# Logits copied out in their own step, the slot sum divided after the experts, a shorter merge of four groups

## The chip, the cores and the metric

The kernel runs on one core of a Trainium2 chip. The metric is device time in microseconds, 398.91 us as the median of three runs before the change. The engines are named as the profile names them: PE (TensorE matmul, with PEld its weight loads), DVE (VectorE), ACT (ScalarE), POOL (GpSimd) and SP (the queue that issues all transfers here).

## What is computed

The reference, cut to what matters (sizes: 4 sequences of 576 tokens, 8 heads of 64, so N = 2304 tokens of width 512; 8 experts with 4 slots each, 32 slots; inner width 1024; feed-forward width 2048):

```python
# attention in a window of 64 tokens, causal; output x: [2304, 512]
logits = x @ phi                                     # [N, 32]
d = exp(logits - logits.max(0)); d /= d.sum(0) + 1e-9   # over the tokens, per slot
slot_input = d.T @ x                                 # [32, 512]
for e in range(8):                                   # 4 slots each
    slot_out[e] = maximum(slot_input[e] @ w1[e], 0) @ w2[e]
c = exp(logits - logits.max(1)); c /= c.sum(1) + 1e-9   # over the slots, per token
y = c @ slot_out                                     # [N, 512]
h = y @ w_in; out = (h * sigmoid(1.702 * h)) @ w_out
```

## The kernel before, in words

**Attention.** A list `work` of 20 steps is run by one loop (line 618), five for each sequence `b`: a step for each of its four pairs of heads and, second among the five, a short one for the tail of the sequence. The loop is a pipeline written out by hand, and every engine executes its own instructions in the order of the program. In pass `i` PE does the scores of step i (`emit_s`, lines 324 and 338), the transposes of step i-1 (`emit_t`, line 359), the transposes of the attention output of step i-2 (`xt_step`, lines 415 and 421) and the product with V of step i-1 (`emit_pv`, line 374). ACT does the exponentials (`emit_e`, line 350) and copies transposes out of PSUM (lines 360 and 430), DVE the row maxima (line 343) and the normalisation (`emit_norm`), POOL scales and shifts inputs as they land (lines 218, 238 and 241).

**Routing.** The softmax over the tokens is built online, one sequence at a time (`routing(b)`), and its parts are hung into the loop by the tables `early` (between `emit_e(i, 0)` and `xt_step`) and `late` (after `emit_e(i, 1)`). For b = 0, 1, 2 the order is: in step 5b + 6, late, `all_logits` (lines 480 to 491) on PE; in step 5b + 7, early, `lmax` on DVE (lines 500 to 505: running maximum and the change of it) and `dexp` on ACT (line 510 the exponential, with its sum; 513; and line 515, a copy of the raw logits into the SBUF strip `ls`); late in the same step `dtr`, which transposes the exponentials and the raw logits on PE (lines 522 and 523); in step 5b + 8 `slots` on PE (539 and 542) and `gather` on DVE, which adds to `acc`. The softmax over the slots (`norm`, `side`) hangs in later.

**PSUM banks.** Eight banks are handed out in rings: `s` three, `v` two, `m` three. `emit_t` takes two of `m` in each step, `xt_step` one, `all_logits` one, `dtr` two, `slots` one. A tile waits until the one that had its bank has been read. In step 5b + 7 the ring gives `xt_step` the bank that `all_logits` took one step before, and the last reader of that bank is the copy in line 515. After the loop the rings are `s` [1, 0], `t` [2, 7], `v` [3, 4], `m` [5, 6].

**The merge.** For the fourth sequence the same is done outside the loop (lines 688 to 742). The partitions of `acc` hold four groups of the 32 slots, each with its own running maximum and sum, and these are merged: PE transposes the maxima (line 701), DVE reduces them, PE spreads the result (708), DVE and ACT make the factor of each group (712 and 713). Then the sums are brought together (717, 719, PE at 721), the reciprocal is taken (722, 724), the factors are made (725, 726), `acc` is scaled (727), the last `slots` are added (734), and PE sums the four groups and transposes in one (738); DVE copies the result, `siT`, which stands in the buffer `phis` (741). Between these stand the parts of `c` for three sequences (`sides[b][0]` to `[2]`: line 439 on PE, 448 on ACT, 453 on DVE).

**Experts and feed-forward.** `emit_w1` (lines 753 and 757) makes four rounds over the 16 tiles of w1, `emit_ht` transposes the hidden values, `emit_w2` (line 792) goes over the 16 tiles of w2, `so_copy` (line 842) copies the sum out of PSUM, `so_turn` (848) transposes it. The feed-forward stage then takes the rest of the time, in 48 steps of matmuls (lines 948 and 975) with the activation on ACT.

**Transfers.** All are issued by SP, in the order of the program, each when its buffer is free: in each attention step one pair's q and k (512 KB), its v (256 KB), and one or two 1 MB tiles of w1; w2 goes first into the space that attention leaves (`arena`), and from the seventh tile on into the slots that a round of `emit_w1` frees.

Of the kernel before, what the change touches and what calls it, by code (L numbers as in the profile page):

```python
# [15 lines left out]
ACTF = mybir.ActivationFunctionType  # L16
ALU = mybir.AluOpType
# [3 lines left out]
B, H, S, D = 4, 8, 576, 64  # L21
# [53 lines left out]
def attention_softmoe_ffn(  # L75
# [12 lines left out]
    nc = tc.nc  # L88
# [12 lines left out]
    pa = s1.tile([128, 2048], F32, tag="pa", name="pa")  # L101
# [7 lines left out]
    def bank(tag, shape=(128, 512), dtype=F32):  # L109
        ring = rings[tag]  # L110
        ring.append(ring.pop(0))
        return psp.tile(list(shape), dtype, tag=f"b{ring[-1]}", name=tag)
# [10 lines left out]
    acc = cst.tile([128, DM], F32, name="acc")  # L123
# [17 lines left out]
    def load_w(n=1):  # L141
        for _ in range(n):
            if plan:
                lst, src, i, d = plan.pop()
                t = wslot() if d is None else dslot(d)
                v = src[i].rearrange("p (a f) -> p a f", a=4)
                for c in HALVES if plan == [] else (slice(0, 512),):
                    nc.sync.dma_start(out=t[:, :, c], in_=v[:, :, c])
                lst.append(t)
# [133 lines left out]
    ls = rawt[:, LS0:LS0 + 192]  # L283
# [11 lines left out]
    i4m = i4.rearrange("p j s -> p (j s)")  # L295
# [141 lines left out]
    def c_tile(p, l):  # L437
        for j in range(4):
            nc.tensor.matmul(
                p[32 * j:32 * j + 32], l, ident, start=True, stop=True, tile_position=(0, 32 * j))  # L440
# [30 lines left out]
    def routing(b):  # L471
        st = {}
# [5 lines left out]
        def logits(lp, kks, rest):  # L478
            if rest:
                nc.tensor.matmul(  # L480
                    lp[:, 128:192], negs[:, 0:128], negs[:, 128:192], start=True, stop=True)
                for kk in range(KD):
                    nc.tensor.matmul(
                        lp[0:32, 128:192], phis[:, kk, :], xT[:, kk, 512:S],
                        start=(kk == 0), stop=(kk == KD - 1), tile_position=(0, 0))
            for kk in kks:
                for t in range(4):
                    nc.tensor.matmul(
                        lp[32 * t:32 * t + 32, 0:128], phis[:, kk, :],
                        xT[:, kk, 128 * t:128 * t + 128],  # L490
                        start=(kk == 0), stop=(kk == KD - 1), tile_position=(0, 32 * t))
            st["lp"] = lp[:, 0:192]

        def all_logits():
            logits(bank("m"), range(KD), True)

        def lmax():

            m = sp.tile([128, 1], F32, tag="mrun", name="mrun")
            nc.vector.tensor_reduce(out=m, in_=st["lp"], axis=AX.X, op=ALU.max, negate=True)  # L500
            if b:
                nc.vector.tensor_tensor(out=m, in0=m, in1=run["m"], op=ALU.min)
                al = sp.tile([128, 1], F32, tag="al", name="al")
                nc.vector.tensor_tensor(out=al, in0=m, in1=run["m"], op=ALU.subtract)
                st["al"] = al
            run["m"] = m

        def dexp():
            s = sp.tile([128, 1], F32, tag="srun", name="srun")
            nc.scalar.activation(  # L510
                out=lt, in_=st["lp"], func=ACTF.Exp, bias=run["m"], scale=1.0, accum_out=s)
            if b:
                nc.scalar.activation(out=st["al"], in_=st["al"], func=ACTF.Exp)
            st["s"] = s
            nc.scalar.copy(ls, st["lp"])  # L515

        d = mem(D0, TB * NS).rearrange("p (t s) -> p t s", t=TB)

# [59 lines left out]
                out=l, in0=l, in1=mc.unsqueeze(2).to_broadcast([128, TB, NS]), op=ALU.mult)  # L578

        def c_turn():  # L580
            st["pq"] = pq = bank("t")
            for t in range(4):
                c_tile(pq[:, 128 * t:128 * t + 128], l[:, t, :])

# [3 lines left out]
        def c_lo():  # L588
            c_low(b * S, st["pq"])

        main = [all_logits, lmax, dexp, dtr, slots, gather, logits, turn]
        norm = [c_max, c_sub, c_exp, c_sum, c_add, c_rec, c_mul]
        side = [c_turn, c_hi, c_lo]
        return st, main, norm, side


    early, late = {}, {}
    sides = []
    for b in range(B - 1):
        _, main, norm, side = routing(b)  # L600
        sides.append(side)
        n = 5 * b
        late[n + 6] = main[0:1]
        early[n + 7] = main[1:3]
        late[n + 7] = main[3:4]
        early[n + 8] = main[4:5]
        late[n + 8] = main[5:6] + norm[0:3]
        late[n + 9] = norm[3:7]
    last, main, norm, side = routing(B - 1)
    sides.append(side)  # L610
    lmax, dexp, slots, logits, turn = (main[k] for k in (1, 2, 4, 6, 7))
# [6 lines left out]
    for i in range(ns + 1):  # L618
        u, b = work[i] if i < ns else (None, None)
# [60 lines left out]
    def warm(n):  # L680
# [15 lines left out]
    m, al = run["m"], last["al"]  # L696
# [3 lines left out]
    pm = bank("s")  # L700
# [3 lines left out]
        out=ml[:, 4, :], in_=pm[0:1, 0:128].rearrange("p (j s) -> p s j", j=4), axis=AX.X,  # L704
        op=ALU.min)
# [4 lines left out]
        start=True, stop=True)  # L710
    rsl = sp.tile([128, 4], F32, tag="rsl", name="rsl")
    nc.vector.tensor_tensor(out=rsl[:, 2:3], in0=pm[:, 128:129], in1=m, op=ALU.subtract)
    nc.scalar.activation(out=rsl[:, 2:3], in_=rsl[:, 2:3], func=ACTF.Exp)
    sides[1][1]()
    sides[0][2]()

    nc.vector.scalar_tensor_tensor(
        out=rsl[:, 3:4], in0=prev_s, scalar=al, in1=last["s"], op0=ALU.mult, op1=ALU.add)
    nc.vector.tensor_tensor(out=rsl[:, 3:4], in0=rsl[:, 3:4], in1=rsl[:, 2:3], op=ALU.mult)
    slots()  # L720
    nc.tensor.matmul(pm[:, 129:130], i4m, rsl[:, 3:4], start=True, stop=True)
    nc.vector.tensor_scalar(
        out=rsl[:, 1:2], in0=pm[:, 129:130], scalar1=1e-9, scalar2=None, op0=ALU.add)
    nc.vector.reciprocal(out=rsl[:, 0:1], in_=rsl[:, 1:2])
    nc.vector.tensor_tensor(out=rsl[:, 0:1], in0=rsl[:, 0:1], in1=rsl[:, 2:3], op=ALU.mult)
    nc.vector.tensor_tensor(out=rsl[:, 1:2], in0=rsl[:, 0:1], in1=al, op=ALU.mult)
    nc.vector.tensor_scalar(
        out=acc, in0=acc, scalar1=rsl[:, 1:2], scalar2=None, op0=ALU.mult)
    load_w(2)
    siT = phis  # L730
    sides[2][0]()
    psi = bank("m", (128, KD, 32))
    for k, c in enumerate(HALVES):
        nc.vector.scalar_tensor_tensor(
            out=acc[:, c], in0=last["pa"][:, c], scalar=rsl[:, 0:1], in1=acc[:, c],
            op0=ALU.mult, op1=ALU.add)
        for kk in (2 * k, 2 * k + 1):
            nc.tensor.matmul(
                psi[:, kk, :], acc[:, kk * 128:kk * 128 + 128], i4m[:, 0:32],
                start=True, stop=True)  # L740
    nc.vector.tensor_copy(siT, psi)  # L741
    sides[2][1]()
    ht = rawt
    nc.gpsimd.memset(ht[:, 0:NE * 260], 0.0)

# [39 lines left out]
    po = bank("v")  # L785
# [51 lines left out]
    so = hsb[0]  # L837
    soT = rawt[:, 0:512].rearrange("p (k s) -> p k s", k=KD)

    def so_copy():  # L840
        for c in HALVES:
            nc.scalar.copy(so[:, c], po[:, c])

    def so_turn(k):

# [163 lines left out]
    for i in range(16):  # L1009
# [17 lines left out]
        for f in ahead.get(i, ()):  # L1027
            f()
    so_copy()
    warm(W[0])  # L1030
    so_turn(0)
# [27 lines left out]
    for n in range(len(steps)):  # L1059
# [3 lines left out]
        if n in more:  # L1063
            b = more[n]
# [80 lines left out]
```

## Time and profile before

| | |
|---|---|
| three runs | 400.89, 394.71, 398.91 us, median 398.91 us |
| the profiled execution | 393.94 us, of it 392.2 us from its first to its last instruction |
| TensorE clock, mean | 0.978 of full |
| PE busy | 372.8 us, 95% of the span |
| DVE, ACT, POOL busy | 243.9, 196.4, 46.4 us (62%, 50%, 12%) |
| chain of work that ended last | PE 84%, ACT 6%, DVE 6%, DMA 2% |
| moved by DMA | 70.84 MB |

Attention runs to about 113 us of the span, the merge to 125, the experts to 160, the feed-forward stage to the end. Matmuls are pipelined, and a busy PE is not a PE at its peak: a matmul at half clock counts as busy like one at full clock, so the granted clock is read beside the busy time.

### The profile page before, as it was taken

To read this page: it belongs to the slowest core of one execution; us is meant where nothing else is said; L and a number is where in the kernel's file an instruction comes from. 1 tells how busy PE (TensorE), PEld (TensorE's weight loads), DVE (VectorE), ACT (ScalarE), POOL (GpSimd) and SP (SyncE) were. 2 spreads that over 40 slices of the span, in tenths; PEclk is the share of its full clock that TensorE was granted. 3 is DMA by queue.
4 is the path that set the end of the run, shared out by engine and by line. 5 is a ranking of instruction groups with operands and counts; after the bars stand their busy time and mean duration, and the time that the engine had idled before them with its cause. 6 is when DMAs were issued, how large, how long until landed. Compare 5 with 4: busy or idle time off the path is not lost.

```text
span 392.2 us, 8119 instructions
## 1 busy us (share of the span) xinstructions
PE 372.8 (95%) x3206; PEld 281.2 (72%) x3206; DVE 243.9 (62%) x556; ACT 196.4 (50%) x504; POOL 46.4 (12%) x80
## 2 busy tenths in 40 slices
PE   8997997997998999999999999999999999999995
PEld 7786585686664343567877888788887788888884
DVE  3556586685844522177948597788869695453624
ACT  2796586586651230347666654555544553334330
POOL 5446345413110000000000000000000000000000
PEclk9999899699997899999999999999999999999999
DMA  8999989779977599613313131404020000012304
GB/s 265 386 389 387 402 294 402 265 264 403 352 250 308 210 424 397 258 56 107 107 55 107 53 117 47 162 4 153 20 92 0 3 0 0 2 65 96 138 24 161
DMA packets 26726, 70.84 MB, mean 181 GB/s; under 512 B 2496, under 2 KB 13760, under 8 KB 22720
## 3 DMA queue, kind: packets, MB, share of 16 engines
q1 hardware_dynamic: 26688, 70.33, 48.8%
q8 instruction: 25, 0.41, 0.4%
q14 instruction: 13, 0.11, 0.1%
HBM read 65.60 MB, written 4.72 MB: 179 GB/s over the span
## 4 chain that ended last, share of the span: by engine, by line
PE 84%; ACT 6%; DVE 6%; DMA 2%; issue 1%; POOL 0%; ACTq 0%; SPq 0%; DVEq 0%; POOLq 0%
PE s L975 16%; PE t L975 16%; PE v L975 16%; PE s L753 4%; PE m L948 4%; PE v L374 4%; PE s L338 4%; PE v L792 4%; PE m L359 3%; ACT pa L360 2%; DMA arena<-in_vt_dram 2%; PE v L259 2%; ACT pa L350 2%; PE s L324 1%; PE m L415 1%
## 5 line engine op out<-in xcount | busy, mean ns | idle before, releaser
L935 ACT ACTIVATE r<-m 128x384 fp32r<-128x384 f32 x96 | 47.3, 494 | 82.9 <-PE m L948 82.9
L962 DVE TENSOR_TENSOR r<-g,r 128x384 fp32r<-128x384 f32 x96 | 51.3, 554 | 50.4 <-ACT g L935 42.3
L975 PE MATMUL t<-w,r 128*128 128x512 f32 x288 | 75.9, 395 | 0.0
L975 PE MATMUL s<-w,r 128*128 128x512 f32 x288 | 74.6, 393 | 0.5 <-DVE r L962 0.5
L975 PE MATMUL v<-w,r 128*128 128x512 f32 x288 | 73.4, 389 | 0.0
L975 PEld LDWEIGHTS t<-w,r 128*128 128x128 f32 x288 | 53.8, 188 | 14.8 <-issue 3.9
L975 PEld LDWEIGHTS v<-w,r 128*128 128x128 f32 x288 | 54.1, 188 | 11.4
L975 PEld LDWEIGHTS s<-w,r 128*128 128x128 f32 x288 | 52.5, 188 | 9.3 <-DVE r L962 0.9
L935 ACT ACTIVATE g<-m 128x384 f32<-128x384 f32 x96 | 47.8, 499 | 0.0
L350 ACT ACTIVATE pa<-s,nm 128x128 f32<-128x128 f32 x144 | 42.3, 395 | 7.0 <-DVE nm L343 6.9
L360 ACT COPY pa<-m 128x512 f32<-128x512 f32 (+1 forms) x40 | 20.1, 552 | 25.0 <-PE m L359 24.9
L343 DVE TENSOR_REDUCE nm<-s 128x4 f32<-128x512 f32 (+1 forms) x40 | 23.6, 631 | 7.6 <-PE s L338 7.2
L948 PE MATMUL m<-cT,w 128*128 128x384 f32 (+2 forms) x112 | 26.0, 322 | 0.6 <-ACT g L935 0.6
L948 PEld LDWEIGHTS m<-cT,w 128*128 128x128 f32 x112 | 20.7, 188 | 5.9 <-ACT g L935 1.7
L359 PE MATMUL m<-ident,pa 128*128 128x128 f32 x144 | 21.7, 290 | 0.2 <-ACT pa L350 0.2
L359 PEld LDWEIGHTS m<-ident,pa 128*128 128x128 f32 x144 | 16.3, 146 | 4.4 <-issue 3.1
L374 PE MATMUL v<-arena,pa 128*64 128x65 f32 x384 | 17.2, 235 | 1.0 <-ACT pa L360 0.3
L374 PEld LDWEIGHTS v<-arena,pa 128*64 128x64 f32 x384 | 13.9, 143 | 4.7 <-ACT pa L360 3.7
L753 PE MATMUL s<-w,phis 128*32 128x512 f32 x128 | 16.9, 673 | 0.5 <-DVE phis L741 0.5
L415 PE MATMUL m<-ident,arena 128*128 128x128 f32 x64 | 10.3, 282 | 7.0 <-ACT rawt L515 6.9
L384 DVE TENSOR_SCALAR rs<-v 128x4 f32<-128x4 f32 (+1 forms) x40 | 5.4, 158 | 15.7 <-PE v L374 15.5
L338 PE MATMUL s<-arena 64*64 64x128 f32 x384 | 14.2, 282 | 0.7 <-POOL arena L218 0.7
(198 smaller groups left out, 460.0 us busy)
## 6 DMA issues: line engine op xcount, KB each, us to landing
w<-in_w_dram SPq DMA_DIRECT2D x24, 1024.0 KB, 10.7
w<-in_w_out_dram SPq DMA_DIRECT2D x16, 512.0 KB, 3.3
arena<-in_w_dram SPq DMA_DIRECT2D x7, 1024.0 KB, 6.3
iraw<-in_w_in_dram SPq DMA_DIRECT2D x12, 512.0 KB, 3.3
arena<-in_qk_dram SPq DMA_DIRECT2D x10, 512.0 KB, 7.7
out_dram<-w SPq DMA_DIRECT2D x16, 256.0 KB, 2.1
rawt<-in_qk_dram SPq DMA_DIRECT2D x6, 512.0 KB, 7.3
arena<-in_vt_dram SPq DMA_DIRECT2D x10, 256.0 KB, 7.5
```

Of the source, the lines that this page charges most:

```text
L338: nc.tensor.matmul(st[h][rows[j], c, :], q, k, start=False, stop=(c == n - 1), tile_position=(64 * h, 64 * j))
L343: nc.vector.tensor_reduce(out=nm[:, h, 0:n], in_=st[h][:, 0:n], axis=AX.X, op=ALU.max, negate=True)
L350: nc.scalar.activation(out=pb[h][:, c, :], in_=st[h][:, c, :], func=ACTF.Exp, bias=nm[:, h, c:c + 1], scale=1.0)
L359: nc.tensor.transpose(tt[:, c, :], pb[h][:, c, :], ident)
L360: nc.scalar.copy(ab[h][:, 0:n], tt[:, 0:n])
L374: nc.tensor.matmul(pvt[i][h][64 * j:64 * j + 64, c, :], ab[h][:, c, 64 * j:64 * j + 64], v, start=True, stop=True, tile_position=(0, 64 * j))
L753: nc.tensor.matmul(ph[32 * j:32 * j + 32, :], siT[:, kk, :], w1t[4 * r + j][:, kk, :], start=(kk == 0), stop=(kk == KD - 1), tile_position ...
L792: nc.tensor.matmul(po[32 * j:32 * j + 32, c], ht[:, e * 256 + fc * 32:e * 256 + fc * 32 + 32], w2t[i][:, j, c], start=(i == 0), stop=(i == ...
L935: nc.scalar.activation(out=(gh, g)[part], in_=ph[:, 0:PIECE], func=ACTF.Gelu_apprx_sigmoid)
L948: nc.tensor.matmul(ph[:, c - a:c - a + m], mst[:, f * 128:f * 128 + 128], cT(c, m), start=True, stop=True)
L962: nc.vector.tensor_tensor(out=gl, in0=g, in1=gh.bitcast(F32), op=ALU.subtract)
L975: nc.tensor.matmul(accs[t], a[:, c], b, start=(first and k == 0), stop=(last and k == 2))
```

## The change

Four edits. In `all_logits` the raw logits are copied to `ls` straight after the matmuls, and `lmax` and `dexp` of b = 0, 1, 2 read `ls` in place of the PSUM bank; for b = 3 the copy stays in `dexp`. `c_turn` of b = 2 takes a bank of ring `v` in place of `t`. In the merge the factors no longer hold the reciprocal of the sum: `acc` is scaled as soon as the groups' factors are there, the four groups' sums and the reciprocal are computed behind the copy of `siT`, and two parts of `c` stand in other places. `so_copy` multiplies by the reciprocal, as a scale of the activation, one number for each partition. Since the experts are linear but for a maximum with zero, and the divisor is positive, dividing behind them gives the same.

```diff
--- before.py
+++ after.py
@@ -493,6 +493,8 @@
 
         def all_logits():
             logits(bank("m"), range(KD), True)
+            nc.scalar.copy(ls, st["lp"])
+            st["lp"] = ls
 
         def lmax():
 
@@ -512,7 +514,8 @@
             if b:
                 nc.scalar.activation(out=st["al"], in_=st["al"], func=ACTF.Exp)
             st["s"] = s
-            nc.scalar.copy(ls, st["lp"])
+            if b == B - 1:
+                nc.scalar.copy(ls, st["lp"])
 
         d = mem(D0, TB * NS).rearrange("p (t s) -> p t s", t=TB)
 
@@ -578,7 +581,7 @@
                 out=l, in0=l, in1=mc.unsqueeze(2).to_broadcast([128, TB, NS]), op=ALU.mult)
 
         def c_turn():
-            st["pq"] = pq = bank("t")
+            st["pq"] = pq = bank("v" if b == B - 2 else "t")
             for t in range(4):
                 c_tile(pq[:, 128 * t:128 * t + 128], l[:, t, :])
 
@@ -711,35 +714,35 @@
     rsl = sp.tile([128, 4], F32, tag="rsl", name="rsl")
     nc.vector.tensor_tensor(out=rsl[:, 2:3], in0=pm[:, 128:129], in1=m, op=ALU.subtract)
     nc.scalar.activation(out=rsl[:, 2:3], in_=rsl[:, 2:3], func=ACTF.Exp)
-    sides[1][1]()
-    sides[0][2]()
-
+
+
+    nc.vector.tensor_tensor(out=rsl[:, 1:2], in0=rsl[:, 2:3], in1=al, op=ALU.mult)
+    nc.vector.tensor_scalar(
+        out=acc, in0=acc, scalar1=rsl[:, 1:2], scalar2=None, op0=ALU.mult)
     nc.vector.scalar_tensor_tensor(
         out=rsl[:, 3:4], in0=prev_s, scalar=al, in1=last["s"], op0=ALU.mult, op1=ALU.add)
     nc.vector.tensor_tensor(out=rsl[:, 3:4], in0=rsl[:, 3:4], in1=rsl[:, 2:3], op=ALU.mult)
+    sides[1][1]()
     slots()
-    nc.tensor.matmul(pm[:, 129:130], i4m, rsl[:, 3:4], start=True, stop=True)
-    nc.vector.tensor_scalar(
-        out=rsl[:, 1:2], in0=pm[:, 129:130], scalar1=1e-9, scalar2=None, op0=ALU.add)
-    nc.vector.reciprocal(out=rsl[:, 0:1], in_=rsl[:, 1:2])
-    nc.vector.tensor_tensor(out=rsl[:, 0:1], in0=rsl[:, 0:1], in1=rsl[:, 2:3], op=ALU.mult)
-    nc.vector.tensor_tensor(out=rsl[:, 1:2], in0=rsl[:, 0:1], in1=al, op=ALU.mult)
-    nc.vector.tensor_scalar(
-        out=acc, in0=acc, scalar1=rsl[:, 1:2], scalar2=None, op0=ALU.mult)
     load_w(2)
     siT = phis
     sides[2][0]()
     psi = bank("m", (128, KD, 32))
     for k, c in enumerate(HALVES):
         nc.vector.scalar_tensor_tensor(
-            out=acc[:, c], in0=last["pa"][:, c], scalar=rsl[:, 0:1], in1=acc[:, c],
+            out=acc[:, c], in0=last["pa"][:, c], scalar=rsl[:, 2:3], in1=acc[:, c],
             op0=ALU.mult, op1=ALU.add)
         for kk in (2 * k, 2 * k + 1):
             nc.tensor.matmul(
                 psi[:, kk, :], acc[:, kk * 128:kk * 128 + 128], i4m[:, 0:32],
                 start=True, stop=True)
     nc.vector.tensor_copy(siT, psi)
+    nc.tensor.matmul(pm[:, 129:130], i4m, rsl[:, 3:4], start=True, stop=True)
+    nc.vector.tensor_scalar(
+        out=rsl[:, 1:2], in0=pm[:, 129:130], scalar1=1e-9, scalar2=None, op0=ALU.add)
+    nc.vector.reciprocal(out=rsl[:, 0:1], in_=rsl[:, 1:2])
     sides[2][1]()
+    sides[0][2]()
     ht = rawt
     nc.gpsimd.memset(ht[:, 0:NE * 260], 0.0)
 
@@ -839,7 +842,8 @@
 
     def so_copy():
         for c in HALVES:
-            nc.scalar.copy(so[:, c], po[:, c])
+            nc.scalar.activation(
+                out=so[:, c], in_=po[:, c], func=ACTF.Copy, scale=rsl[:, 0:1])
 
     def so_turn(k):
 
```

## Rows read from the trace of the kernel before

**Rows 1.** Waits of PE, 20 to 116 us: us in total, times, longest.

```profile
PE m L415 <- ACT rawt L515: 6.9, 3, 2.3
```

**Rows 2.** Stretches: length, busy PE, PEld, DVE, ACT, POOL, clock, DMA, GB/s.

```profile
36.05:49.44 13.39, 11.16 (x157) 7.38 (x155) 7.75 (x23) 7.07 (x24) 6.67 (x9) 0.87 1.02 394
63.73:78.76 15.03, 12.71 (x156) 8.53 (x154) 9.22 (x25) 7.85 (x26) 6.92 (x9) 0.77 0.81 306
92.19:104.27 12.08, 9.76 (x156) 6.40 (x156) 7.42 (x24) 7.20 (x25) 2.72 (x5) 1.00 0.96 353
```

**Rows 3.** Timeline (start, length; idle before in brackets), step 17.

```profile
93.40 0.66 PE L359 MATMUL m<-ident,pa 128*128 128x128 f32 x4
...
93.93 0.65 ACT L360 COPY pa<-m 128x256 f32<-128x256 f32 x2 [2.81 <-PE m L359]
...
95.49 0.45 ACT L510 ACTIVATE arena<-m,mrun 128x192 f32<-128x192 f32 x1
...
95.81 0.22 ACT L510 ACTIVATION_READ_ACCUMULATOR arena<-m,mrun 128x1 f32 x1
...
95.99 0.33 ACT L515 COPY rawt<-m 128x192 f32<-128x192 f32 x1
...
96.38 0.66 PE L415 MATMUL m<-ident,arena 128*128 128x128 f32 x4 [2.32 <-ACT rawt L515]
...
97.58 0.33 PE L522 MATMUL m<-ident,arena 128*128 128x128 f32 x1
```

**Rows 4.** Timeline, end of step 6 and start of step 7.

```profile
34.83 0.74 ACT L160 ACTIVATE wi<-w 128x512 f32<-128x512 f32 x1
...
35.09 1.04 PE L488 MATMUL m<-arena,phis 128*32 128x128 f32 x29
...
37.80 0.65 ACT L360 COPY pa<-m 128x256 f32<-128x256 f32 x2 [2.23 <-PE m L359]
```

**Rows 5.** Timeline of the merge and the first two rounds of the experts.

```profile
118.32 0.20 ACT L713 ACTIVATE rsl<-rsl 128x1 f32<-128x1 f32 x1 [0.76 <-DVE rsl L712]
...
119.17 1.04 PE L542 MATMUL m<-arena 64*32 64x512 f32 x2
...
120.28 0.38 PE L721 MATMUL s<-rsl,i 128*128 128x1 f32 x2
...
120.59 1.08 PE L439 MATMUL t<-ident,lg 128*32 128x128 f32 x32
...
121.48 0.48 DVE L727 TENSOR_SCALAR acc<-acc,rsl 128x512 f32<-128x512 f32 x1
...
122.00 0.88 DVE L734 SCALAR_TENSOR_TENSOR acc<-m,rsl,acc 128x256 f32<-128x256 f32 x2
...
122.64 1.76 PE L738 MATMUL m<-i,acc 128*128 128x32 f32 x8 [0.96 <-DVE acc L734]
124.44 0.29 DVE L741 COPY phis<-m 128x128 f32<-128x128 f32 x1 [1.55 <-PE m L738]
...
124.87 5.96 PE L753 MATMUL s<-w,phis 128*32 128x512 f32 x32 [0.47 <-DVE phis L741]
...
131.17 3.64 PE L753 MATMUL s<-w,phis 128*32 128x512 f32 x32
```

**Rows 6.** Merge end and first expert round, columns as in rows 2.

```profile
122.80:129.60 6.80, 6.33 (x32) 2.81 (x35) 0.37 (x2) 0.00 (x0) 0.00 (x0) 0.50 0.60 252
```

**Rows 7.** Stretch around step 13 and 14, columns as in rows 2.

```profile
72.00:82.00 10.00, 9.92 (x138) 6.88 (x132) 8.84 (x21) 5.22 (x16) 3.74 (x5) 0.85 0.48 171
```

**Rows 8.** Timeline: a load of q and k is scaled, and its first use.

```profile
47.19 0.62 POOL L218 TENSOR_SCALAR arena<-arena 128x512 f32<-128x512 f32 x1 [5.30 <-DMA arena<-in_qk_dram]
...
54.12 1.17 PE L338 MATMUL s<-arena 64*64 64x128 f32 x32
```

**Rows 9.** Timeline: ACT in the experts' stage and at its end.

```profile
136.15 1.28 ACT L775 ACT_TABLE_LOAD   x1
...
160.18 0.65 ACT L842 COPY acc<-v 128x256 f32<-128x256 f32 x2 [12.93 <-PE v L792]
```

## The prediction

> **What bounds the kernel now.** I read the shares of busy time first: PE works in 95% of the span and carries most of the chain that ended last, so only what PE waits for, or does slowly, is worth anything. The waits of PE in attention come next [rows 1]: the one of any size is that of `xt_step` (line 415) on the copy in line 515, three times, 6.9 us together. PE being busy says nothing of its clock, so I then compared the same work three times over [rows 2]: the stretch from the scores of step 5b + 7 to the scores of step 5b + 9, for b = 0, 1, 2. It takes 13.39, 15.03 and 12.08 us, at a mean granted clock of 0.87, 0.77 and 1.00 of full. The levels are 1.2 and 2.4 GHz, so 0.77 means 0.46 of 15.03 us, 6.9 us, at the lower one, and half of that, 3.5 us, as loss, near the 2.95 us by which this pass is longer than the third. The wait costs twice: as idle time, and then, in two passes of three, as a slower PE. The end of the merge is such a place too: 122.8 to 129.6 us ran at 0.50 [rows 6], and in it the first round of the experts took 5.96 us, the second, with the same matmuls, 3.64 [rows 5].
>
> **Edit 1, the copy.** Where PE waits, the timeline of step 17 shows what it waits for [rows 3]. The transposes of line 359 end at 94.06. Line 415 is independent of the new sequence but gets the bank that the logits hold until line 515 is through at 96.32, and that stands on ACT behind the exponential and its sum, which stand behind DVE's maximum. With the copy in the step before, the bank is free, and line 415 starts at 94.06. From its start to the next transposes (line 522) PE needed 1.20 us (96.38 to 97.58), so it comes there at 95.26. There it has a new wait, and this is what is late next: line 522 reads the exponentials, whose sum is through at 96.03. With the 0.06 us that lay between line 515 and line 415, it starts at 96.09 in place of 97.58. The gain is 1.49 us a pass, not 2.32, and 0.83 us of idle time stays. All that follows on PE moves up by as much. Bounds: nothing, if something else holds line 415; 2.32, if line 522 comes with no wait. I take 1.49, since every term of it stands in one pass.
>
> The copy itself, 0.33 us of ACT, is not removed but moved to the end of the step before. Cover: ACT idles 2.81 us there before its next copy (line 360) [rows 3]. In the first pass a conversion of 0.74 us (line 160) stands behind it [rows 4]: the logits end at 36.13, copy and conversion at about 37.2, and line 360 is due at 37.80. Nobody waits, with 0.6 us to spare; with that gone, each 0.1 us beyond is one on PE. `lmax` and the exponential read SBUF in place of PSUM; I leave their lengths alone.
>
> If the clock holds in all three passes, each takes what the third takes less the gain, 12.08 - 1.49 = 10.59, together 31.8 against 40.5: **8.7 us**. If the clock falls as it did, only 3 x 1.49 = 4.5 remain. Between these I take the first: the idle time that led to the falls shrinks from 2.3 to 0.8 us, and in the third pass even 2.32 us brought no fall.
>
> **Edit 2, the bank of `c_turn`.** Ring `t` then has no tile of b = 0 in the way of b = 2, so DVE's two subtractions for b = 0 (`sides[0][2]`) can go from ahead of the sums to behind line 741. There DVE's next work waits for a whole round of experts, 3.64 us at least [rows 5]: nothing. The next user of ring `v` is the sum of w2, and it gets the other bank.
>
> **Edit 3, the merge** [rows 5]. Before, after `slots` end at 120.21, the sums go through PE (line 721, 0.38 us) and five small instructions of DVE; `acc` is scaled until 121.96; line 734 starts at 122.00; PE runs line 738 from 122.64 to 124.40; DVE copies; the experts start at 124.87. After, ACT's factor is there at 118.52, one product and the scaling (0.48) are done before 119.3, while PE is in `slots`. Line 734 can run at 120.25, its second half done at 121.15. PE goes on with the turn for b = 2 (1.08 us) from 120.21 to 121.29, which is now the later of the two, then line 738 for 1.76 and the 0.47 us to the experts: 123.52, **1.35 us** earlier. The sums' matmul, 0.38 us, falls into the 0.47 in which PE waits for `siT`. Its DVE instructions are needed only by `so_copy`, 35 us later. No transfer is passed: `load_w(2)` waits, as before, for `slots`.
>
> If the clock holds here as well, the first round takes 3.64 in place of 5.96 (2.32 less) and line 738 half of 1.76 (0.88 less): 1.35 + 2.32 + 0.88 = **4.55 us**. Bounds 1.35 and 4.55. I take the upper: the 0.96 us of idle time before line 738, and what lay around line 721, are gone.
>
> **Edit 4, the scaled copy.** Two copies of 256 columns on the path [rows 9]. The nearest price for an operand of one number per partition is the exponential, which has one, against the copy of the same 192 columns, which has none: 0.45 and 0.33 us [rows 3], 0.12 more, for two 0.24. Bounds 0 and 0.24, since nothing in it is faster; I take 0.2, as the second is partly behind PE. If a scaled copy needed another table, two loads of 1.28 us [rows 9] would come on the path. The Trainium skill (ScalarE: Activation LUTs, section Table sets: the hidden batching unit) says that copy is among the functions of every set, which would make it none; no trace shown here has a scaled copy to check it.
>
> **The sum** against the profiled execution: 393.94 - 8.7 - 4.55 + 0.2 = 380.9 us. That execution lies 0.8 us under the fastest of the three runs and 5.0 under their median. Three passes at the 15.03 us of the second would cost 4.6 us more than these three did, so I read the spread of the runs as clock that falls in more or fewer places; what causes it would go as well. I add the 0.8: **382 us**.
>
> **Rivals.**
> *The clock still falls.* For: I cannot tell from these rows how much idle time it takes, and the merge fell with less than 1 us before line 738. Against: pass three. If it falls in the merge alone, 393.94 - 8.7 - 1.35 + 0.2 = 384.1; if in all three places as before, 393.94 - 4.5 - 1.35 + 0.2 = 388.3; with the 0.8, 385 to 389.
> *The loads hold the steps back.* For: DMA is busy in nearly all of attention (1.02 and 0.96 in two of the passes [rows 2]). Against: around steps 13 and 14 the share was 0.48 over 10 us [rows 7], 5.2 us unused, because SP itself waits for PE to free buffers and so moves up with it; and the load that was waited for longest was scaled at 47.81 and used at 54.12 [rows 8], 6.3 us later, while PE is then only 2.8 us ahead (13.39 less 10.59). If only the first pass and the merge gained: 393.94 - 2.8 - 4.55 + 0.2 + 0.8 = 387.6. The tiles of w2 follow the experts' first round, and DMA had 40% free there [rows 6].
> *The table load.* 2 x 1.28 more: 384.6.
> *Slower: the experts stay at 1.2 GHz.* They now begin after a different stretch of work. Between the second round and the scaled copy lie 29 us (131.17 to 160.18), and a round at low clock takes 5.96 / 3.64 = 1.64 times as long, so 18.5 us more on the case without clock: 388.3 + 18.5 + 0.8 = 407.6. It decides from 9 us at low clock on (5.6 / 0.64). Against: the second round ran at full rate with the same matmuls.
> *The edit does not free the bank.* The copy ends some 0.4 us after the logits, line 415 wants the bank after a whole `emit_s`; I give it no share.
>
> **Chances.** Forecast 0.65, the clock 0.20, the loads 0.08, the table 0.04, slower 0.03. About 2%, 8 us, can be told from no change. Against the median, 391 is the border, against the fastest run 387: the forecast and the table lie under both, of the clock's 0.20 I count 0.11 as faster, of the loads' 0.08 0.03. Faster 0.83, within 2% 0.14, slower 0.03. The low end is the sum without the 0.8 and with no idle time left in the passes, 380.9 - 2.5 = 378.4; the high end takes in the clock and the loads, 389.5.
>
> **What would show it.** In the profile after: no wait of PE on line 515; line 522 waiting under 1 us on line 510; the three stretches at about 10.6 us and clock 1.00; the experts starting 3 us after `slots` end, and their first round near 3.6 us. Wrong if the stretches differ by the clock again, if line 338 or 374 waits for POOL, or if line 753 starts late by a wait on DVE.

## The result, and the profile after

| | before | after |
|---|---|---|
| runs, us | 400.89, 394.71, 398.91, 394.01 | 380.63, 384.75, 381.03, 381.34 |
| median, us | 396.81 | 381.18 |
| profiled execution, us | 393.94 | 380.63 |
| TensorE clock of it, mean | 0.978 | 0.998 |

The change makes the kernel faster: ratio 0.9648, with a 95% interval of 0.954 to 0.9756. The medians here and below are over all runs of a kernel, the ratios leave disturbed runs out. Where one time stands "beside" another, the other is the median of the runs of before that were made together with the kernel in question. The lines have moved: the copy is line 496 (518 for b = 3), line 510 is now 512, 522 is 525, 712 and 713 are 715 and 716, 721 is 740, 734 is 732, 738 is 736, 741 is 739, 753 is 756, 842 is 845, 542 is 545, 727 is 720, 848 is 852. The kernels of the experiments have line numbers of their own, and their rows show these.

The answer to [rows 2], the three stretches from scores to scores (columns: window and its length, then busy us and count of PE, PEld, DVE, ACT and POOL, granted clock, DMA share, GB/s):

```profile
35.76:46.38 10.62, 9.72 (x157) 6.51 (x155) 7.74 (x23) 7.85 (x25) 4.77 (x6) 1.00 1.03 395
60.57:71.17 10.60, 9.70 (x156) 6.49 (x154) 8.35 (x25) 7.47 (x26) 5.44 (x7) 1.00 1.04 398
84.82:95.62 10.80, 9.71 (x157) 6.51 (x156) 7.45 (x24) 7.34 (x25) 2.56 (x5) 1.00 1.01 373
```

Read the second number and the third from the end together: three equal stretches, all at full clock, in place of 13.39, 15.03 and 12.08 us at 0.87, 0.77 and 1.00. The page's row of the clock over the whole span, in 40 slices and in tenths of full, has the dents of before in its first line, and none in the second, which is that of after:

```profile
PEclk9999899699997899999999999999999999999999
PEclk9999999999999999999999999999999999999999
```

The answer to [rows 1] and [rows 3], step 17 in the timeline (start, length, what it is, idle time ahead of it and what ended that):

```profile
84.98 0.32 ACT L496 COPY rawt<-m 128x192 f32<-128x192 f32 x1 [1.22 <-PE m L488]
...
86.05 0.65 PE L359 MATMUL m<-ident,pa 128*128 128x128 f32 x4
86.54 0.60 PE L415 MATMUL m<-ident,arena 128*128 128x128 f32 x4
...
88.33 0.46 ACT L512 ACTIVATE arena<-rawt,mrun 128x192 f32<-128x192 f32 x1
88.69 0.19 ACT L512 ACTIVATION_READ_ACCUMULATOR arena<-rawt,mrun 128x1 f32 x1
...
88.93 0.33 PE L525 MATMUL m<-ident,arena 128*128 128x128 f32 x1 [1.09 <-ACT arena L512]
```

The copy is done at 85.30, before the transposes of line 359 begin, line 415 follows line 359 with no bracket behind it, and the wait that is left is on line 525, for the exponential. PE's largest waits from 20 to 108 us (engine, tile, line, releaser; sum, count, longest) say the same of all three passes:

```profile
PE m L525 <- ACT arena L512: 2.9, 3, 1.1
PE s L338 <- POOL arena L218: 1.2, 1, 1.2
```

The second of them, on POOL, is not new. From 20 to 116 us before had it too, a little shorter:

```profile
PE s L338 <- POOL arena L218: 0.7, 1, 0.7
```

The answer to [rows 5], the merge:

```profile
109.88 0.48 DVE L720 TENSOR_SCALAR acc<-acc,rsl 128x512 f32<-128x512 f32 x1
...
110.31 1.04 PE L545 MATMUL m<-arena 64*32 64x512 f32 x2
...
111.28 1.08 PE L439 MATMUL v<-ident,lg 128*32 128x128 f32 x32
111.39 0.88 DVE L732 SCALAR_TENSOR_TENSOR acc<-m,rsl,acc 128x256 f32<-128x256 f32 x2 [0.70 <-PE m L545]
...
112.29 1.08 PE L736 MATMUL m<-i,acc 128*128 128x32 f32 x8
...
113.20 0.36 PE L740 MATMUL s<-rsl,i 128*128 128x1 f32 x2
113.41 0.29 DVE L739 COPY phis<-m 128x128 f32<-128x128 f32 x1 [1.14 <-PE m L736]
...
113.84 3.64 PE L756 MATMUL s<-w,phis 128*32 128x512 f32 x32 [0.28 <-DVE rsl L741]
```

`acc` is scaled (line 720) before `slots` (line 545) end, PE has no wait ahead of line 736, the sums (line 740) lie in the gap ahead of the experts, and the first round takes the 3.64 us that only the second took before [rows 5].

### The profile page after: what moved, and what is told of

Read it like the earlier page. It is cut to its first block, busy times and chain, and to the rows that moved or that the text cites. A ratio compares the mean times of both kernels' runs of the same rounds, so it can differ in the third digit from the quotient of the medians.

```text
span 378.9 us, 8123 instructions
## 1 busy us (share of the span) xinstructions
PE 364.4 (96%) x3206; PEld 276.9 (73%) x3206; DVE 242.8 (64%) x555; ACT 196.6 (52%) x504; POOL 47.5 (13%) x80
## 4 chain that ended last, share of the span: by engine, by line
PE 85%; DVE 5%; ACT 5%; DMA 3%; issue 1%; POOL 1%; ACTq 0%; POOLq 0%; SPq 0%
PE s L979 17%; PE t L979 17%; PE v L979 16%; PE m L952 4%; PE s L756 4%; PE v L795 4%; PE s L338 4%; PE v L374 3%; PE m L359 3%; DMA arena<-in_qk_dram 3%; PE v L259 2%; ACT pa L360 2%; PE s L324 2%; ACT pa L350 1%; PE m L542 1%; PE m L545 1%
## 5 line engine op out<-in xcount | busy, mean ns | idle before, releaser
L359 PE MATMUL m<-ident,pa 128*128 128x128 f32 x144 | 20.9, 283 | 0.2 <-ACT pa L350 0.2
L374 PE MATMUL v<-arena,pa 128*64 128x65 f32 x384 | 16.4, 228 | 1.0 <-ACT pa L360 0.3
L756 PE MATMUL s<-w,phis 128*32 128x512 f32 x128 | 14.5, 594 | 0.3 <-DVE rsl L741 0.3
L338 PE MATMUL s<-arena 64*64 64x128 f32 x384 | 13.4, 270 | 1.2 <-POOL arena L218 1.2
L998 DVE TENSOR_TENSOR w<-s,w 128x512 f32<-128x512 f32 x18 | 11.6, 684 | 2.8 <-PE s L979 2.8
```

The costliest lines, as they stand in the source:

```text
L338: nc.tensor.matmul(st[h][rows[j], c, :], q, k, start=False, stop=(c == n - 1), tile_position=(64 * h, 64 * j))
L359: nc.tensor.transpose(tt[:, c, :], pb[h][:, c, :], ident)
L374: nc.tensor.matmul(pvt[i][h][64 * j:64 * j + 64, c, :], ab[h][:, c, 64 * j:64 * j + 64], v, start=True, stop=True, tile_position=(0, 64 * j))
L756: nc.tensor.matmul(ph[32 * j:32 * j + 32, :], siT[:, kk, :], w1t[4 * r + j][:, kk, :], start=(kk == 0), stop=(kk == KD - 1), tile_position ...
```

## Experiments

The theory of the prediction (A in the expectations) has two halves: the change returns 4.5 + 1.35 us in which PE stood, and, because PE no longer stands long, the clock that fell at those places. The rival is that the clock falls for another reason, or that one edit carries the gain alone. Measured against the 2% that the prediction set as the border, after, after_again, e4, e4b, e7 and e8 are faster than before, e2 is the same, and the intervals of e1, e3, e5 and e6 lie across the border. What these last five show is therefore read from their traces first, and from their times second.

**e1_copy_only: before, with edit 1 alone.**

```diff
+            nc.scalar.copy(ls, st["lp"])      # in all_logits
+            st["lp"] = ls
...
+            if b == B - 1:                    # in dexp
                 nc.scalar.copy(ls, st["lp"])
```

> The copy of the logits alone moved into its own step; the merge, the banks and the division as before. Theory A (the wait on the copy costs idle time and, through it, the clock): the three stretches of steps 5b+7 and 5b+8 take 10.6 to 10.8 us each at clock 1.00, 8.5 us less than before, and the line 522 wait of 0.8 to 1.1 us is there; the merge still loses about 1 us of PE ahead of line 738, and if that idle time is what took the clock, the first round of experts takes 6 us again: 385.5 us. Rival B (whether the clock falls depends on where in time the work lies, not on the idle time): stretches between 10.6 and 13 us, clock below 1 in one or two of them, and the merge may keep its clock: 382 to 390 us.

390.0, 390.49, 384.55 and 384.43 us: median 387.27 beside 396.07, ratio 0.9744 (0.9644 to 0.9844). The profiled execution is one of the long ones, and its stretches show why:

```profile
35.73:46.33 10.60, 9.69 (x155) 6.48 (x154) 7.67 (x22) 7.74 (x25) 5.05 (x6) 1.00 1.03 394
60.63:71.24 10.61, 9.70 (x156) 6.49 (x155) 8.34 (x26) 7.48 (x26) 5.16 (x7) 1.00 1.05 400
85.24:97.69 12.45, 11.33 (x157) 7.94 (x155) 7.50 (x23) 7.36 (x25) 2.72 (x5) 0.86 0.87 320
```

Two stretches as in after; in the third the clock fell to 0.86. Its timeline there:

```profile
89.38 0.33 PE L525 MATMUL m<-ident,arena 128*128 128x128 f32 x1 [1.12 <-ACT arena L512]
...
90.44 1.93 PE L338 MATMUL s<-arena 64*64 64x128 f32 x32
```

The scores of line 338 take 1.93 us behind a wait of 1.12 us. In after the same wait was 1.09 us, and the clock stayed. So the wait that edit 1 leaves lies where the clock may fall or not, and on its three stretches alone this run speaks for rival B as much as for A, which asked for a clock of 1.00 in all of them; the two runs of 384.5 had a mean clock of 0.995, the two of 390 one of 0.986. The merge, which edit 1 leaves alone, still had its wait of 0.96 us ahead of the last product, and the clock fell there again, as A has it:

```profile
122.05 4.86 PE L756 MATMUL s<-w,phis 128*32 128x512 f32 x32 [0.47 <-DVE phis L744]
```

Earlier, at the start of the merge, PE stood once where it waited for nothing that the profile shows ("issue"), in the middle of line 439:

```profile
106.51 1.05 PE L439 MATMUL t<-ident,lg 128*32 128x128 f32 x30
110.74 0.46 PE L439 MATMUL t<-ident,lg 128*32 128x128 f32 x2 [3.18 <-issue]
```

The DMA view of 107.5 to 111 us (queue, kind: packets, MB, share) has one transfer of instructions in it:

```profile
q8 instruction: 1, 0.02, 1.7%
```

Such transfers are in every execution, 25 or 26 of them on this queue, so one that merely lies near a stand says little. But this one is late. In before it begins at 111.00, 2.07 us ahead of the first matmul of line 439 (113.07); in after, after_again, e2, e4, e6, e7 and e8 it is 1.9 to 2.3 us ahead as well. Here it begins at 108.43, 1.92 us behind that matmul, and PE goes on 2.31 us later.

**e2_merge_only: after, without edit 1** (the diff above, taken back).

> The merge, the banks and the scaled copy as after; the copy of the logits back in the exponential's place. Theory A: the three stretches as in the kernel before (12.1 to 15 us each, 6.9 us of waits on the copy), and only the merge is shorter: the experts start about 2.5 us after the slots end, their first round takes 3.64 us: 4.4 us less than before, about 389.5 us. Rival B: the merge's clock falls as before, and only 1.2 us are gained: 392.8 us.

391.99, 391.59, 392.36 and 390.88 us, median 391.79, ratio 0.988 (0.9819 to 0.9941). The stretches:

```profile
36.73:51.69 14.96, 12.72 (x157) 8.47 (x154) 7.69 (x22) 7.13 (x24) 6.72 (x9) 0.77 0.92 357
66.01:79.80 13.79, 11.27 (x155) 7.61 (x154) 8.52 (x25) 7.78 (x26) 6.18 (x8) 0.88 0.87 334
93.18:106.89 13.71, 11.38 (x156) 7.75 (x155) 7.46 (x23) 7.17 (x25) 2.72 (x5) 0.88 0.83 310
```

All three fell, the third too: they take 42.46 us together, where before took 40.50, and that is most of the 2.3 us by which the forecast of 389.5 was missed. From the end of `slots` (122.63) to the experts (125.12) it is 2.49 us, as in after, at full clock. The two halves add up within their intervals: 2.6% and 1.2%, against 3.5% for both.

**e3_fill_wait: before, with work in the wait.** The wait on line 515 stays; eight matmuls of 128 columns, whose result nobody uses, keep PE at work in it.

```diff
...
+        if i in (7, 12, 17):                  # ahead of xt_step
+            pvt[i - 1] = [bank("v", (128, 4, 65)) for _ in range(2)]
+            fill = pvt[i - 1][0].rearrange("p c k -> p (c k)")[:, 0:128]
+            for _ in range(8):
+                nc.tensor.matmul(fill, ident, ident, start=True, stop=True)
```

> The kernel before with eight idle-filling matmuls of 128 columns on PE ahead of line 415 in steps 7, 12 and 17 only: the wait on the copy stays as long, but PE works in it. Theory A: the clock holds in all three stretches, each takes about 12.1 us as the third did before, 4.3 us less in all: about 389.6 us, with the merge as before. Rival B (the fall has another cause than idle PE): stretches of 13.4 and 15 us stay, no gain, about 394 us, or more if the added matmuls are on the path.

388.33, 388.85, 390.47 and 386.53 us, median 388.59, ratio 0.9802 (0.9718 to 0.9886). This is the run that tells the theories apart: not an instruction that the step needs comes earlier, and yet

```profile
35.77:47.77 12.00, 11.55 (x172) 8.24 (x171) 7.87 (x22) 7.13 (x24) 5.71 (x8) 1.00 1.03 394
62.16:74.27 12.11, 11.56 (x173) 8.24 (x172) 8.26 (x26) 7.50 (x26) 6.11 (x8) 1.00 0.96 374
88.20:100.30 12.10, 11.56 (x172) 8.24 (x170) 7.40 (x23) 7.21 (x25) 2.75 (x5) 1.00 0.87 325
```

all three run at full clock. In the first of them the filling (which the trace records as 16 matmuls) stands where PE had 2.23 us of idle time, and line 415, here 416, still goes on only when the copy is through:

```profile
37.48 1.95 PE L635 MATMUL v<-ident 128*128 128x128 f32 x16
39.88 0.66 PE L416 MATMUL m<-ident,arena 128*128 128x128 f32 x4 [0.45 <-ACT rawt L516]
```

The mean of the three stretches, 12.07 us, is 1.40 above the 10.67 of after: that is the price of the wait by itself, forecast at 1.49. The merge, where nothing was filled, still fell (first round 5.34 us).

**e5_fill_all: the same, and three more matmuls on `ident` ahead of line 738** (`warm(3)`, which the trace records as six).

> The kernel before with filling matmuls on PE in the three waits on the copy and three more (128 columns) ahead of line 738 in the merge; every wait stays as long, none of the four edits is in. Theory A (idle PE ahead of the experts is what takes the clock in the merge): the clock is at 1.00 from the start to the end of the feed-forward, the first round of experts takes 3.64 us, 1.7 to 2.4 us less than with the three waits filled: 386 to 387 us. Rival B (the matmuls of the merge are too thin to hold the clock, idle or not): the first round takes 5 to 6 us as before, 388.5 us.

386.7, 386.58, 386.65 and 387.42 us, median 386.67 beside 394.38, ratio 0.9809 (0.9761 to 0.9857). From 10 to 380 us the clock is 1.00:

```profile
10.00:380.00 370.00, 362.75 (x3190) 275.77 (x3189) 237.57 (x536) 193.66 (x499) 40.53 (x55) 1.00 0.49 181
```

and the merge, with the filling (line 688) ahead of its last product, keeps it:

```profile
117.56 0.94 PE L688 MATMUL v<-ident 128*128 128x128 f32 x6
118.59 1.05 PE L745 MATMUL m<-i,acc 128*128 128x32 f32 x8
120.12 3.64 PE L760 MATMUL s<-w,phis 128*32 128x512 f32 x32 [0.48 <-DVE phis L748]
```

Clock alone is worth 394.38 - 386.67 = 7.7 us, or 1.9% of the 3.5% by which after is faster. The idle time is the rest, and its size is less certain: 386.67 - 381.18 = 5.5 us by the medians, 1.6% or 6.3 us by the ratios, 386.70 - 380.63 = 6.1 us by the profiled executions, but only 386.67 - 383.38 = 3.3 us against the runs of after_again, which were made beside this kernel.

The spread goes too: 0.84 us over four runs, where eleven runs of before beside it reach from 390.9 to 396.34. Four runs are few (those of e2_merge_only spread by 1.48 us with nothing filled), but the clock of the eleven says the same. As an estimate, a run loses its span times (1 - mean clock) to the lower level, since half of the time there is loss; for the run of 394.38 us that is 392.6 x 0.022 = 8.6 us. With it taken off, all eleven lie between 385.5 and 387.4 us, around the 386.67 of the filled kernel.

**e6_divide_first: after, with the reciprocal and its product back between `slots` and the scaling of `acc`**, and a plain copy in `so_copy`. The two subtractions (`sides[0][2]`) stay behind; `sides[1][1]` is back in its old place in the program, which leaves the order on ACT as it is in after.

```diff
     slots()
+    nc.tensor.matmul(pm[:, 129:130], i4m, rsl[:, 3:4], start=True, stop=True)
...
+    nc.vector.reciprocal(out=rsl[:, 0:1], in_=rsl[:, 1:2])
...
+    nc.vector.tensor_scalar(
+        out=acc, in0=acc, scalar1=rsl[:, 1:2], scalar2=None, op0=ALU.mult)
```

> The kernel after with the division put back ahead of the experts: the sums go through PE and DVE (matmul, reciprocal, two products) before the scaling of acc, and the copy at the end is plain; the two subtractions stay behind, the bank of the turn stays. Theory A (the division is what lengthens the path): the experts start 3.7 to 4 us after the slots end in place of 2.5, 1.3 us later, 0.1 less at the plain copy: 381.8 us where the kernel after has 380.6; with the 1 us of idle time the clock may fall in the merge again, 1.6 to 3.2 us more. Rival D (moving the subtractions was the gain): no change, 380.6 us.

385.03, 390.39, 387.28 and 386.29 us, median 386.78, ratio 0.9819 (0.9759 to 0.988). The merge on PE:

```profile
111.79 1.04 PE L545 MATMUL m<-arena 64*32 64x512 f32 x2
...
115.11 1.05 PE L741 MATMUL m<-i,acc 128*128 128x32 f32 x8 [0.96 <-DVE acc L737]
116.64 5.34 PE L757 MATMUL s<-w,phis 128*32 128x512 f32 x32 [0.47 <-DVE phis L744]
```

The 0.96 us of [rows 5] is back, 3.81 us lie between `slots` and the experts, and the round behind takes 5.34 us in place of 3.64. 1.32 + 1.70 = 3.0 of the 4.4 us by which this execution is longer than the one of after; 1.5 us were lost ahead of the merge (`slots` end at 112.83, in after at 111.35). That part is not the division's: in after_again, whose code is that of after, `slots` end at 113.19.

**e7_sub_ahead: after, with DVE's two subtractions for b = 0 ahead of the scaling again.**

```diff
     nc.scalar.activation(out=rsl[:, 2:3], in_=rsl[:, 2:3], func=ACTF.Exp)
+    sides[0][2]()
...
     sides[2][1]()
-    sides[0][2]()
```

> The kernel after with the two subtractions of b = 0 put back ahead of the scaling of acc, 1.4 us of DVE; all else as after. Theory A (PE's turn for b = 2 covers them, edit 2 is worth nothing by itself): the experts start 2.5 to 2.8 us after the slots end, the time is that of the kernel after, 381 to 382.5 us in undisturbed runs. Rival D (DVE is on the path of the merge): the scaling of acc ends 1.4 us later, the experts start 3.5 us or more after the slots, 1 us more.

381.48, 382.89, 387.25 and 381.37 us, median 382.18, ratio 0.9681 (0.9615 to 0.9747), which includes that of after. From `slots` to the experts 2.66 us, 0.17 more: so moving the subtractions, which edit 2 makes possible, is worth no more than that. The bank itself was taken back in no run that has the new merge.

**e4_max_early: after, with `lmax` and `dexp` of b = 0, 1, 2 a step earlier**, at the end of step 5b + 6, so that line 525 does not wait.

```diff
-        early[n + 7] = main[1:3]
+        tail[n + 6] = main[1:3]
...
         load_w(W_AT.get(i, 0))
+        for f in tail.get(i, ()):
+            f()
```

> The kernel after with the maximum and the exponential of b = 0, 1, 2 emitted at the end of step 5b+6, behind the normalisation, in place of behind the exponentials of step 5b+7. Theory A (what is left of the wait is the order on DVE and ACT: the maximum stands behind the row maxima): line 525 no longer waits, each stretch takes 9.8 us in place of 10.6 to 10.8, 2.5 us less: about 378.5 us. Rival C (ACT or DVE is the bound once the wait is gone): line 360's copies or the row maxima come later by 0.5 us or more, and PE waits for them in place of line 525: 380.5 to 382 us.

378.27, 378.61, 382.89 and 381.76 us, median 380.19, ratio 0.9594 (0.9516 to 0.9673). The stretches have no idle time left in the first two:

```profile
35.96:45.73 9.77, 9.77 (x157) 6.63 (x155) 7.69 (x22) 7.78 (x25) 5.02 (x6) 1.00 1.03 396
60.03:69.62 9.59, 9.59 (x158) 6.46 (x155) 8.23 (x25) 7.37 (x25) 4.32 (x5) 1.00 1.04 395
83.39:93.27 9.88, 9.78 (x157) 6.50 (x155) 7.50 (x24) 7.24 (x25) 2.97 (x5) 1.00 1.04 395
```

To settle the distance to after, both ran once more side by side.

**after_again:**

> The kernel after once more, beside the next one on the same chip: 380.5 to 382 us in most runs. One profile so far (the copy alone) showed PE standing 3.2 us for nothing that the trace names, with a transfer of its instructions under way; if that is what lifts single runs, some runs of this kernel lie 3 to 5 us above the others at nearly the same clock.

382.48, 381.06, 381.65, 385.51, 385.18 and 384.28 us, median 383.38, ratio 0.972 (0.9671 to 0.977). Three runs lie at 381.06 to 382.48 us, with a mean clock of 0.999 or 1.000, and three at 384.28 to 385.51, with 0.994 or 0.995. The profiled one is that of 382.48 us: the clock did not fall in it before the end, but step 7 begins at 37.02, 1.26 us later than in the first profile of after (35.76), before the first of the edits has acted.

**e4b_max_early:**

> The maximum and the exponential early, again, beside the kernel after: 2.4 us less than it, run for run, since line 525 no longer waits (378.3 against 380.6 us). Rival: the 2.4 us were chance between calls, and both have the same median.

383.48, 378.81, 379.89, 379.9, 387.11, 387.69 and 379.64 us, median 379.9, ratio 0.9623 (0.9568 to 0.9679). The intervals of the two touch, so the gain, 3.5 us by these medians and 1.0 by those of the first runs, is likely and not settled. The execution of 383.48 us shows what goes wrong in such a run, in PE's waits from 18 to 122 us:

```profile
PE m L415 <- issue: 1.9, 1, 1.9
PE s L338 <- POOL arena L218: 1.9, 1, 1.9
```

The first is a stand without a releaser, at 105.5 to 107.4, and again a transfer of instructions is late: it begins at 104.88, 0.44 us behind the first matmul of line 439 and not 2 us ahead of it, and PE goes on 2.55 us later. The clock fell behind both waits.

**e8_loads_later: e4_max_early, with the first tiles of w1 asked for three steps later**, so that q and k come first.

```diff
-W_AT = {i: 1 for i in range(2, 18)}
+W_AT = {i: 2 if i in (9, 13, 14) else 1 for i in range(5, 18)}
```

> The early maximum and exponential, and the tiles of w1 of steps 2 to 4 loaded in steps 9, 13 and 14 instead. Rival of the prediction (the loads hold the steps back) in its place: with three 1 MB tiles fewer ahead of it, the q and k of step 5 land earlier, and PE no longer waits 1.0 to 1.9 us for POOL at the scores of step 6: 377 to 378 us in undisturbed runs, where the early maximum alone has 378.3 to 379.9. If the wait stays, the loads ahead of step 6 are not w1.

377.26, 381.21, 379.55 and 379.02 us, median 379.28, ratio 0.9631 (0.9563 to 0.9699). PE's waits now begin with

```profile
PE v L374 <- issue: 0.5, 1, 0.5
PE v L374 <- ACT pa L360: 0.3, 1, 0.3
```

The wait on POOL is gone from this profile; of the eleven others, all with the loads as before, ten had 0.5 to 1.9 us of it and e5_fill_all none, so this one profile makes the loads likely and does not settle it. In time that is at most the 1 us between 378.27 and 377.26, the two profiled executions. All three sets of runs with the early maximum are far below before and, by 1 to 4 us in their medians, below those of after.

## Why the prediction was right

The sum said 380.9 us for the profiled execution, which took 380.63; the forecast of 382 lies 0.8 above the median of the first four runs of after and 1.4 below that of the six of after_again. That the sum came within 0.3 us is in part luck. Its three terms measure 8.48 + 4.49 - 0.11 = 12.86 us, where it had 13.05, and 0.45 us came from elsewhere, of it 0.29 ahead of step 7 (36.05 to 35.76), which no edit touches.

- **Line 415.** It no longer waits, and line 525 waits 0.90, 0.90 and 1.09 us where 0.83 was foreseen as "what is late next". The three stretches are 32.02 us, so the gain is 8.48 against 8.7. How much of it is clock is shown by e3_fill_wait, whose stretches are 36.21 us: 4.29 us are clock, and 4.19, or 1.40 for each pass, are idle time (1.49 foreseen).
- **The copy's cover.** In the first pass the copy runs from 35.92 to 36.24, the conversion of line 160 until 36.95, and line 360 comes at 37.52 (37.80 in [rows 4]) with 0.58 us of idle time left (0.6 forecast). Nobody waited.
- **The merge.** From the end of `slots` to the experts 2.49 us (4.66 before). The terms of the sum give 4.66 - 1.35 - 0.88 = 2.43; the 3 us among the signs of the prediction do not follow from them. To the end of the first round it is 6.13 against 10.62, a gain of 4.49 (4.55). Line 736 took 1.08 us and not 0.88: the one term of it that was off by a fifth. The experts' first round is put down to DVE's line 741 here, but it starts 0.14 us behind the end of the copy (113.70 to 113.84), as it did before (124.73 to 124.87), so that sign of being wrong did not come. e6_divide_first shows that the order of the division is what does it, e7_sub_ahead that moving the subtractions costs nothing, as forecast.
- **The scaled copy.** 0.84 us for two against 0.65 [rows 9], so 0.19 more (0.24 was the upper bound). PE starts 0.53 us behind the start of the first and not 0.42, so 0.11 are on the path; 0.2 was taken:

```profile
146.83 0.84 ACT L845 ACTIVATE acc<-v,rsl 128x256 f32<-128x256 f32 x2 [12.94 <-PE v L795]
...
147.36 1.16 PE L852 MATMUL t<-i,acc 128*128 128x128 f32 x8
```

 There is no table load ahead of it: the trace agrees with what the Trainium skill (ScalarE: Activation LUTs, section Table sets: the hidden batching unit) was cited for, and that rival falls.
- **The loads.** "Wrong if line 338 or 374 waits for POOL": line 338 did, 1.2 us in step 6 against 0.7 before. But this wait ends at 30.76, before the first copy that the change moves (35.92), and the kernels without edit 1 have it too (1.20 us in e2_merge_only, 1.29 in e3_fill_wait). The sign was badly chosen: the wait varies by itself, and the rival of the loads did not come, since the stretches moved up in full.
- **Where the reason was too strong.** The prediction held that 0.8 us of idle time would keep the clock, because 2.32 us had left it alone in one pass. But in e2_merge_only that third pass fell as well, the clock fell behind waits of 1.12 us (e1_copy_only) and 0.96 us with 0.47 behind it (e6_divide_first), and did not behind waits of 1.09 us (after) and of 1.2 us on POOL (after, e2_merge_only). That it held in every place of the profiled execution of after is in part luck: four of the ten runs of after have a mean clock of 0.994 or 0.995, where the others have 0.998 to 1.000, and one fall like that in e1_copy_only costs about that much (0.14 of 12.45 us is 1.7 us, 0.0046 of the span). The chance of 0.20 for "the clock still falls" was, if anything, too small. That the spread of the runs is mostly clock, which the prediction read from one pair of passes, is shown by e5_fill_all and by the clock of the runs beside it.

Left open: why a transfer of instructions comes late. A late one together with one fall of the clock would fit the runs of after at 384 to 386 us, but none of these was profiled. What decides whether a gap of about 1 us costs the clock is open too.

## What to carry to other kernels

Price a wait of TensorE twice, as the time that it stands and as the matmuls behind it at half clock; here the second part was the larger by e5_fill_all (1.9% of 3.5%). Whether a gain is clock or idle time can be told by filling the wait with matmuls that nobody uses. A division that commutes with what follows belongs where nobody waits for it, and a buffer's last reader ahead of a chain that does not need it.

## What was not expected

- Filling the gaps takes nearly all of the spread out of the runs: 0.84 us over four runs instead of 5.4 over eleven, with no other change.
- PE stood several times with no releaser in the profile, and a late transfer of instructions fits each time. The twelve profiles have six such stands of 0.4 us or more between 10 us of the span and the experts: 3.18 us (e1_copy_only), 1.93 and 0.80 (e4b_max_early), 1.07 (e5_fill_all), 0.52 (after_again) and 0.46 (e8_loads_later). Each ends 2.3 to 2.6 us after such a transfer begins. Behind the two longest the clock fell, behind the other four it did not.
